# Attention units of 128 tokens: the first four computed whole, the later ones as two chunks of 64

## The chip, the cores and the metric

The kernel runs on one core of one Trainium2 chip. The core has a matrix engine (PE, with its weight loads shown apart as PEld), a vector engine (DVE), a scalar engine (ACT), a general engine (POOL) and queues that issue transfers (SP's and ACT's are used here). The metric is the device time of one execution in microseconds (us).

## The reference

Three stages follow each other. In the attention stage (4 sequences of 576 tokens, 8 heads of 64), each head's score matrix is multiplied by a fixed mask that decays with distance, and there is no softmax. The 2304 rows of its output then pass through two feed-forward layers of width 2048, one with SiLU and one with a squared ReLU.

```python
scores = scale * np.matmul(q, k.transpose(0, 1, 3, 2))
Dmat = np.where(rel >= 0, gamma[:, None, None] ** rel[None, :, :], 0.0)
x = np.matmul(scores * Dmat[None, :, :, :], v)     # then (tokens, 512)
h = x @ moe_w_in;  x = (h / (1 + np.exp(-h))) @ moe_w_out
h = np.maximum(x @ moe2_w_in, 0.0);  out = (h * h) @ moe2_w_out
```

Since the mask is a power of the distance, the attention of a chunk of tokens is a masked product inside the chunk plus the query times a state, a 64x64 matrix for each head that sums the decayed keys times values of all chunks before it in the sequence.

## The kernel before

**Feed-forward.** Weights and activations are split into a high and a low part, and each product is three matmuls (`mm3`, L74). Tokens go in five blocks of 512, 384, 384, 512 and 512. For each layer, block j and slice f of 16, `gemm1` makes `ph`, `gate` makes `gh` (ACT) and `gl` (DVE, L448), and `gemm2` of the slice two iterations earlier adds to `acc`. The work stands in the order in which the main loop (L561 to L598) writes it. Each iteration has two halves, and what is put in `later` is written at the next `flush`, one half on.

**Weights.** The first layer's 32 weight parts are converted on the chip while block 0 runs. One step of `conv_to` works on three parts: `conv_c` (ACT, L121), `conv_a` (ACT, L101 and L102), `conv_b` (DVE, L107 to L109) and `conv_d` (DVE, L125, `wl`). Five steps lie in the startup, and the main loop writes two for each iteration of block 0, ahead of that half's `flush`. The second layer's weights are converted in the same way much later.

**Attention.** The 18 units of 128 tokens (L is 64, C is 128) are all computed alike. `scores` makes `P` with 16 matmuls for the 64x64 tiles of the matrix engine, 128 columns each (L257). `mask` multiplies `P` by the table `Tm` into `rf` (DVE, L265, 1024 columns). `scale_q` (POOL, L273, two operations) multiplies the query by decay factors, and `decayed_state` multiplies the old state (POOL, L287). `values` adds into `Q` the query times the old state (8 matmuls, L306, 64x64 tiles, 128 columns), the masked scores times the values (8 matmuls, L306, all 128 rows, 128 columns), and the new part of the state (8 matmuls, L325, 64 columns). `high` copies to `xh` (ACT, L333), `new_state` adds the state (DVE, L294), and `low` makes `xl` (DVE, L333). `prep_k` multiplies the keys by a table before L325 reads them, on ACT with 8 operations (L247), in the first four units half on POOL. A matmul of 32-bit data leaves two records in the trace.

A sequence has nine chunks of 64, so a unit can span two sequences. `place` gives a chunk's place in its sequence. At place 0 there is no state yet, and at place 8 none has to be handed on. Unit 4 has places 8 and 0, unit 13 likewise; units 8 and 17 end on place 8; unit 9 begins on place 0.

Units 0 to 3 lie in the startup (`first_units`, an order written out by hand). Of the other 14, units 4 to 6 lie between the matmuls of block 0, and 7 to 17 between those of blocks 1 to 3. Each comes as two visits in the matrix engine's order, `scores_step` and, some halves later, `values_step`, which also writes `prep_k` of the next unit. `prep_k` of unit 4 alone is written by the main loop, at i equal to 2 (L573). `P` and `Q` of these units share one PSUM buffer.

Of the kernel before, what the change touches and what calls it, by code (L numbers as in the profile page):

```python
# [7 lines left out]
F32 = mybir.dt.float32  # L8
# [7 lines left out]
B, H, S, D = 4, 8, 576, 64  # L16
NT, DM, DFF = B * S, H * D, 2048
C = 128
# [20 lines left out]
def kernel(  # L39
# [118 lines left out]

    x_t = {}
    block_of = []
    for j, n in enumerate(BLOCKS):
        block_of += [(j, i * C) for i in range(n // C)]

# [1 line left out]
    raw = {}  # L168
    rf_t = {}
    S_at = {}  # L170
    FOUR = ((0, 0), (1, 1), (0, 1), (1, 0))

    cs = cp.tile([128, 1024 + 512 + 8 + 4 + 4], F32, name="cs")
    dummy = cp.tile([128, 1], F32, name="dummy")
    tabs = cs[:, 0:1024], cs[:, 1024:1536]
    Tm = tabs[0].rearrange("p (a e t) -> p e a t", a=4, e=2)
    Tq = tabs[1].rearrange("p (a t) -> p a t", a=4)
    Tkn, dec, gam = cs[:, 1536:1544], cs[:, 1544:1548], cs[:, 1548:1552]

    def load_consts(part):  # L180
        c0, n = ((12, 1024), (12 + 1024, 512))[part]
        nc.scalar.dma_start(out=tabs[part], in_=cst[:, c0 : c0 + n])

    def cut_consts(part):


        if part == 0:
            last = tabs[0].rearrange("p (h t) -> p h t", h=8)[:, :, C - 1]
            nc.scalar.activation(Tkn, last, ACTF.Copy, scale=8.0)
        else:  # L190
            nc.scalar.activation(gam, Tq[:, :, 1], ACTF.Copy, scale=8.0)
            for a in range(4):
                nc.scalar.activation(Tq[:, a], Tq[:, a], ACTF.Copy, scale=gam[:, a : a + 1])
            nc.scalar.activation(dec, Tq[:, :, C - 1], ACTF.Copy, scale=8.0)

    ap_ctx = ExitStack()
    ap = ap_ctx.enter_context(tc.tile_pool(name="ap", bufs=4))
# [3 lines left out]
    def att_psum(startup, name):  # L201
        pool, tag = ps_a, "a"
        if startup:
            pool, tag = [(ps_a, "a"), (ps_s, "s"), (ps_s, "s"), (ps_s, "s")][ps_n[0] % 4]
            ps_n[0] += 1
        return pool.tile([128, 2, 512], F32, tag=tag, name=name)
# [10 lines left out]
            for g in range(NG):  # L217
                queue.dma_start(out=raw[u][g], in_=att[NG * u + g])

    def dims(u, a, e, first, t0, t1):  # L220

        c0 = first + a % 2 * C
        return raw[u][a // 2][HALF[e], c0 + t0 : c0 + t1]

    def toks(u, a, e, first, p):

        c0 = first + (2 * a + e) % 4 * D
        return raw[u][a // 2][p, c0 : c0 + D]

    def place(u, b):  # L230

        return (2 * u + b) % PER

    def own(u):

        return slice(0, C) if place(u, 1) else HALF[1]
# [12 lines left out]
    P_of, Q_of = {}, {}  # L249

    def scores(u, startup):
        P_of[u] = P = att_psum(startup, "P")
        for a in range(4):
            for e, b in FOUR:
                o = P[HALF[b], e, a * C : a * C + C]
                k, q = dims(u, a, e, 768, b * L, b * L + L), dims(u, a, e, 0, 0, C)
                mm(o, k, q, start=True, stop=True)  # L257

    def mask(u):
        if u < n_start:  # L260
            rf = wp.tile([128, 1024], F32, tag="w", name="rf")
        else:
            rf = ap.tile([128, 1024], F32, tag="rf", name="rf", bufs=1)
        rf_t[u] = rf = rf.rearrange("p (e a t) -> p e a t", e=2, a=4)
        nc.vector.tensor_mul(rf, P_of.pop(u).rearrange("p e (a t) -> p e a t", a=4), Tm)  # L265
        if place(u, 1) == 0:
            nc.gpsimd.memset(rf[HALF[0], :, :, L:C], 0.0)

    def scale_q(u):
        if place(u, 0):  # L270
            for g in range(NG):
                q = raw[u][g][:, 0:256].rearrange("p (a t) -> p a t", a=2)
                nc.gpsimd.tensor_mul(q, q, Tq[:, 2 * g : 2 * g + 2])  # L273

    def scores_step(u):
        scores(u, False)
        mask(u)
        scale_q(u)
        decayed_state(u)

    def decayed_state(u):

        if place(u, 1) == PER - 1:
            return
        S_at[u + 1] = new = ap.tile([128, 4, D], F32, tag="S", name="S", bufs=2)
        if place(u, 0) and place(u, 1):
            nc.gpsimd.tensor_mul(new, S_at[u], dec.unsqueeze(2).to_broadcast([128, 4, D]))  # L287

    def new_state(u):
        if place(u, 1) == PER - 1:  # L290
            return
        new, add = S_at[u + 1], Q_of[u][:, 1, 0:256].rearrange("p (a d) -> p a d", a=4)
        if place(u, 0) and place(u, 1):
            nc.vector.tensor_add(new, add, new)  # L294
        else:
            nc.vector.tensor_copy(new, add)

    def values(u, startup):

        Q_of[u] = Q = att_psum(startup, "Q")  # L300
        o = Q[:, 0].rearrange("p (a t) -> p a t", a=4)
        kv = Q[:, 1, 0:256].rearrange("p (a d) -> p a d", a=4)
        started = set()

        def add(e, w, a, b, last):
            mm(w, a, b, start=e not in started, stop=last)  # L306
            started.add(e)

        parts = ((0, C),) if place(u, 1) else ((0, L), (L, C))
        if place(u, 0):  # L310
            t1 = parts[0][1]
            for a in range(4):
                for e in range(2):
                    add(e, o[HALF[e], a, 0:t1], S_at[u][HALF[e], a], dims(u, a, e, 0, 0, t1), False)
        rf = rf_t.pop(u)
        for a in range(4):
            for e in range(2):
# [3 lines left out]
        if place(u, 1) < PER - 1:  # L321
            p = own(u)
            for a in range(4):
                for e in range(2):
                    mm(kv[HALF[e], a], toks(u, a, e, 256, p), toks(u, a, e, 512, p), start=True, stop=True)  # L325
# [5 lines left out]
        xh, xl = (x[:, :, t0 : t0 + C] for x in x_t[j])  # L331
        raw.pop(u)
        return lambda: nc.scalar.copy(xh, o), lambda: nc.vector.tensor_sub(xl, o, xh)  # L333

    def values_step(u):
        high, low = values(u, False)
        later.append(lambda: (high(), new_state(u), later.append(low)))
        if u + 1 < NU:
            prep_k(u + 1)
        load(u + 2)  # L340

    def first_units():


        high, low = {}, {}

        def val(u):
            high[u], low[u] = values(u, True)

        cut_consts(0)  # L350
        cut_consts(1)
        conv_a(0)
        scores(0, True)
        mask(0)
        decayed_state(0)
        prep_k(0)
        conv_b(0)
        val(0)
        conv_c(0)
        conv_d(0)  # L360
        conv_a(1)
        new_state(0)
        high[0]()
        conv_b(1)
        low[0]()
        prep_k(1)
        scores(1, True)
        scale_q(1)
        mask(1)
        decayed_state(1)  # L370
        conv_c(1)
        conv_d(1)
        scores(2, True)
        val(1)
        scale_q(2)
        prep_k(2)
        conv_a(2)
        new_state(1)
        high[1]()
        mask(2)  # L380
        decayed_state(2)
        low[1]()
        conv_b(2)
        scores(3, True)
        val(2)
        scale_q(3)
        prep_k(3)
        new_state(2)
        high[2]()
        mask(3)  # L390
        decayed_state(3)
        conv_c(2)
        low[2]()
        conv_a(3)
        val(3)
        load(n_start, nc.scalar)
        conv_d(2)
        new_state(3)
        high[3]()
        conv_b(3)  # L400
        low[3]()
        conv_a(4)
        conv_n[0] = 5


    g_t = {}
# [105 lines left out]


    nb = len(BLOCKS)
    u_end = [sum(BLOCKS[: j + 1]) // C for j in range(nb)]
# [138 lines left out]
```

## Time and profile before

| | us |
|---|---|
| runs | 880.62, 881.86, 882.60 |
| median | 881.86 |
| profiled execution | 883.38 |
| its span, first to last instruction | 881.4 |
| PE busy in it | 867.9 (98%) |
| DVE busy | 368.8 (42%) |
| ACT busy | 351.5 (40%) |
| POOL busy | 38.5 (4%) |

The span of the profiled execution is 2.0 us shorter than its time, and its time is 1.5 us above the median. A busy PE is a mean over the whole span; the stages differ, and what an engine waited for has to be read in each of them. The startup ends at about 28.7 us, block 0 runs to 127.5, blocks 1 to 4 of the first layer follow, and attention ends at 381.5.

### The profile page before, as it was taken

Reading aid. Unit: us, or ns where it says so; the run is one execution under the profiler, and the core shown is the slowest. Engines: PE = TensorE matmul, PEld = TensorE weight load, DVE = VectorE, ACT = ScalarE, POOL = GpSimd, SP = SyncE. Lnnn points to the kernel's source line nnn. Section 1 sums busy time; section 2 is a strip of 40 time slices with the busy share of each in tenths; the row PEclk is TensorE's granted clock in tenths of the full one; section 3 lists DMA queues with packets and bytes.
Section 4 is the critical chain, followed back from the end, with each engine's and each line's share of the span. In section 5 each row is a group of like instructions: output and inputs, shape, how many; then the busy total and the mean of one; then the engine's idle time right before and its main releaser. Section 6 shows DMA issues by size and latency. Waiting matters only on the chain.

```text
span 881.4 us, 12560 instructions
## 1 busy us (share of the span) xinstructions
PE 867.9 (98%) x5186; PEld 747.7 (85%) x5186; DVE 368.8 (42%) x590; ACT 351.5 (40%) x705; POOL 38.5 (4%) x55
## 2 busy tenths in 40 slices
PE   7999999999999999999999999999999999999998
PEld 5878889999999888888888888899999888888886
DVE  4799972212222222115666777532233332323222
ACT  5687863223242222325565656322222222222221
POOL 3101100000000010000000000000000000000000
PEclk8999999999999999999999999999999999999999
DMA  9555621112112113004323432020020010001001
GB/s 349 188 181 196 223 96 48 48 49 84 49 49 94 39 49 120 1 1 147 140 97 107 175 129 80 0 84 1 1 84 1 1 67 17 1 1 48 1 1 48
DMA packets 21656, 68.17 MB, mean 77 GB/s; under 512 B 2400, under 2 KB 4192, under 8 KB 21216
## 3 DMA queue, kind: packets, MB, share of 16 engines
q1 hardware_dynamic: 16272, 54.14, 17.0%
q10 hardware_dynamic: 5328, 13.24, 4.2%
q8 instruction: 40, 0.66, 0.3%
q14 instruction: 16, 0.13, 0.0%
HBM read 57.93 MB, written 9.44 MB: 76 GB/s over the span
## 4 chain that ended last, share of the span: by engine, by line
PE 94%; DVE 0%; ACT 0%; issue 0%
PE acc L74 45%; PE ph L74 44%; PE Q L306 3%; PE P L257 2%; PE Q L325 1%; DVE gl L448 0%; DVE y L490 0%; ACT y L488 0%
## 5 line engine op out<-in xcount | busy, mean ns | idle before, releaser
L74 PE MATMUL ph<-xh,wh 128*128 128x512 f32 (+2 forms) x648 | 238.6, 368 | 0.0
L74 PE MATMUL ph<-xh,wl 128*128 128x512 f32 (+2 forms) x648 | 237.3, 366 | 0.0
L74 PE MATMUL ph<-xl,wh 128*128 128x512 f32 (+2 forms) x648 | 237.1, 366 | 0.0
L448 DVE TENSOR_TENSOR gl<-sg,gh 128x512 fp32r<-128x512 f32 (+1 forms) x160 | 104.3, 652 | 205.1 <-ACT gh L447 205.1
L74 PEld LDWEIGHTS ph<-xh,wh 128*128 128x128 f32 x648 | 121.6, 188 | 17.4 <-issue 0.7
L74 PEld LDWEIGHTS ph<-xl,wh 128*128 128x128 f32 x648 | 121.7, 188 | 15.8
L74 PEld LDWEIGHTS ph<-xh,wl 128*128 128x128 f32 x648 | 121.7, 188 | 14.8
L443 DVE SCALAR_TENSOR_TENSOR sg<-ph,sg 128x512 f32<-128x512 f32 (+1 forms) x80 | 51.0, 638 | 198.4 <-ACT sg L442 198.4
L442 ACT ACTIVATE sg<-ph 128x512 f32<-128x512 f32 (+1 forms) x80 | 44.4, 555 | 211.7 <-PE ph L74 210.0
L440 ACT ACTIVATE sg<-ph 128x512 f32<-128x512 f32 (+1 forms) x80 | 44.3, 554 | 202.2 <-PE ph L74 202.2
L74 PE MATMUL acc<-gl,wh 128*128 128x512 f32 (+1 forms) x320 | 118.5, 370 | 1.8 <-DVE gl L448 1.8
L74 PE MATMUL acc<-gh,wh 128*128 128x512 f32 (+1 forms) x320 | 119.9, 375 | 0.0
L74 PE MATMUL acc<-gh,wl 128*128 128x512 f32 (+1 forms) x320 | 118.3, 370 | 0.0
L447 ACT CAST gh<-sg 128x512 fp32r<-128x512 f32 (+1 forms) x160 | 92.4, 578 | 53.2 <-DVE sg L443 50.6
L74 PE MATMUL acc<-wh,gl 128*128 128x512 f32 x288 | 112.7, 391 | 0.0
L74 PE MATMUL acc<-wl,gh 128*128 128x512 f32 x288 | 112.6, 391 | 0.0
L74 PE MATMUL acc<-wh,gh 128*128 128x512 f32 x288 | 112.0, 389 | 0.0
L74 PEld LDWEIGHTS acc<-gh,wh 128*128 128x128 f32 x320 | 60.3, 189 | 9.8 <-issue 1.7
L74 PEld LDWEIGHTS acc<-gl,wh 128*128 128x128 f32 x320 | 60.4, 189 | 9.6 <-DVE gl L448 2.3
L74 PEld LDWEIGHTS acc<-gh,wl 128*128 128x128 f32 x320 | 60.5, 189 | 7.8
L74 PEld LDWEIGHTS acc<-wh,gl 128*128 128x128 f32 x288 | 54.0, 188 | 11.4
L74 PEld LDWEIGHTS acc<-wh,gh 128*128 128x128 f32 x288 | 54.1, 188 | 10.4
(46 smaller groups left out, 652.0 us busy)
## 6 DMA issues: line engine op xcount, KB each, us to landing
wr<-w SPq DMA_DIRECT2D x64, 512.0 KB, 3.5
raw<-att SPq DMA_DIRECT2D x32, 512.0 KB, 4.3
x<-y ACTq DMA_DIRECT2D x12, 256.0 KB, 4.4
xr<-x ACTq DMA_DIRECT2D x3, 1024.0 KB, 4.8
out<-y SPq DMA_DIRECT2D x10, 256.0 KB, 2.2
out<-y ACTq DMA_DIRECT2D x7, 256.0 KB, 2.3
x<-y ACTq DMA_DIRECT2D x8, 192.0 KB, 2.0
xr<-x ACTq DMA_DIRECT2D x2, 768.0 KB, 4.3
```

Source lines behind the costliest of these rows:

```text
L74: mm(o, a, b, start=first and i == 0, stop=last and i == n - 1)
L257: mm(o, k, q, start=True, stop=True)
L306: mm(w, a, b, start=e not in started, stop=last)
L325: mm(kv[HALF[e], a], toks(u, a, e, 256, p), toks(u, a, e, 512, p), start=True, stop=True)
L440: nc.scalar.activation(s, ph, ACTF.Silu)
L442: nc.scalar.activation(s, ph, ACTF.Relu)
L443: nc.vector.scalar_tensor_tensor(s, ph, 0.0, s, op0=ALU.max, op1=ALU.mult)
L447: nc.scalar.copy(gh, s)
L448: later.append(lambda: nc.vector.tensor_sub(gl, s, gh))
```

## The change

Units 0 to 3 keep the form they had, in functions of their own (`unit_scores`, `unit_mask`, `unit_scale_q`, `unit_decayed`, `unit_values`, `unit_state`). Units 4 to 17 are computed as two chunks of 64. All their matmuls have 64 rows, 64 columns of weights and 64 columns of data. In `scores` there are 16 for `P` and up to 16 more for the state's new parts, which stood in `values`. In `values` there are up to 16 with the two chunks' states and 16 with the masked scores. `FOUR` is the order in which the four tiles of the matrix engine are used.

`mask` has 512 columns instead of 1024. A unit has two `new_state` additions on DVE, and between them the decayed state `dS` on POOL. Half of the masked products goes to `x1`, which ACT copies out (`xs`) and DVE adds back in two operations on 64 partitions (`whole`), before `xh` is made. In units 4 to 6 `prep_k` now has its first half on POOL. The tables of 64 are cut on ACT by six operations (`cut_consts(2)`). One step of `conv_to` is written ahead of the first gates, at the end of `first_units`.

```diff
 def prep_k(u):
     for g in range(NG):
-        w = Tkn[:, 4 * g : 4 * g + 4]
-        if g == 0 and u < n_start:
+        w = (Tkn_u if u < n_start else Tkn)[:, 4 * g : 4 * g + 4]
+        if g == 0 and u < u_end[1]:
...
 def scores(u, startup):
     for a in range(4):
         for e, b in FOUR:
-            o = P[HALF[b], e, a * C : a * C + C]
-            k, q = dims(u, a, e, 768, b * L, b * L + L), dims(u, a, e, 0, 0, C)
-            mm(o, k, q, start=True, stop=True)
+            o = P[HALF[b], e, a * L : a * L + L]
+            mm(o, dims(u, a, e, b, 768), dims(u, a, e, b, 0), start=True, stop=True)
+    for a in range(4):
+        for e, b in FOUR:
+            if place(u, b) < PER - 1:
+                o = P[HALF[e], b, 256 + a * D : 256 + a * D + D]
+                mm(o, toks(u, a, e, b, 256), toks(u, a, e, b, 512), start=True, stop=True)
...
+def new_state(u, b):
+    n, i = place(u, b), 2 * u + b
+    if n == PER - 1:
+        return
+    new = ap.tile([128, 4, D], F32, tag="S", name="S", bufs=3)
+    add = P_of[u][:, b, 256:512].rearrange("p (a d) -> p a d", a=4)
+    if n == 0:
+        nc.vector.tensor_copy(new, add)
+    else:
+        nc.vector.tensor_add(new, add, dS[0])
+    S_at[i + 1] = new
+    if n + 1 < PER - 1:
+        dS[0] = ap.tile([128, 4, D], F32, tag="dS", name="dS", bufs=1)
+        nc.gpsimd.tensor_mul(dS[0], new, dec.unsqueeze(2).to_broadcast([128, 4, D]))
...
 def scores_step(u):
     scores(u, False)
     mask(u)
     scale_q(u)
-    decayed_state(u)
+    new_state(u, 0)
+    later.append(lambda: new_state(u, 1))
...
 def values(u, startup):
+    for b in range(2):
+        if place(u, b):
+            for a in range(4):
+                for e in range(2):
+                    sg = S_at[2 * u + b][HALF[e], a]
+                    add(e, o[HALF[e], a, b * L : b * L + L], sg, dims(u, a, e, b, 0), None, False)
     for a in range(4):
-        for e in range(2):
-            for t0, t1 in parts:
-                v = toks(u, a, e, 512, slice(0, C))
-                add(e, o[HALF[e], a, t0:t1], v, rf[:, e, a, t0:t1], a == 3 and t1 == C)
...
+        for e, b in FOUR:
+            v = toks(u, a, e, b, 512)
+            if e == b:
+                add(e, o[HALF[e], a, b * L : b * L + L], v, rf[HALF[b], e, a], None, a == 3)
+            else:
+                mm(x1[HALF[e], a], v, rf[HALF[b], e, a], start=True, stop=True)
+    xs = ap.tile([128, 4, L], F32, tag="xs", name="xs", bufs=1)
+    nc.scalar.copy(xs, x1)
+    def whole():
+        for e, p in enumerate(HALF):
+            b = 1 - e
+            oc = o[p, :, b * L : b * L + L]
+            if place(u, b):
+                nc.vector.tensor_add(oc, oc, xs[p])
+            else:
+                nc.vector.tensor_copy(oc, xs[p])
+        nc.scalar.copy(xh, o)
+    return whole, lambda: nc.vector.tensor_sub(xl, o, xh)
...
     conv_n[0] = 5
+    conv_to(0, 6)
+    cut_consts(2)
```

What this moves is shown at three places. PE at the first visit of unit 4, before the change (`L257` are the scores, `[waits ...]` names whose signal a row waits for):

```order
L257 MATMUL P<-raw 64x128 [waits DMAHW5_49]
L257 MATMUL P<-raw 64x128 x7
L257 MATMUL P<-raw 64x128 [waits DMAHW6_49]
L257 MATMUL P<-raw 64x128 x7
L74 MATMUL acc<-gh,wh 128x512 [waits Activation_49]
L74 MATMUL acc<-gl,wh 128x512 [waits DVE_49]
```

The first `gemm2` follows the scores at once. The same place on PE in the changed kernel (`L265` are the scores, `L270` the new parts of the state):

```order
L265 MATMUL P<-raw 64x64 [waits DMAHW5_49]
L265 MATMUL P<-raw 64x64 x7
L265 MATMUL P<-raw 64x64 [waits DMAHW6_49]
L265 MATMUL P<-raw 64x64 x7
L270 MATMUL P<-raw 64x64 [waits Pool_49]
L270 MATMUL P<-raw 64x64 x3
L270 MATMUL P<-raw 64x64 [waits Activation_49]
L270 MATMUL P<-raw 64x64
L270 MATMUL P<-raw 64x64 [waits Activation_49]
L270 MATMUL P<-raw 64x64
L74 MATMUL acc<-gh,wh 128x512
```

The new parts of the state moved into this visit, with waits for POOL and ACT, whose work is `prep_k` of unit 4.

ACT from the second of the first two gates (`L440`, `L447`) to `prep_k` of unit 4 (`L247`), before the change; `L121`, `L101` and `L102` are one step of the conversion:

```order
L440 ACTIVATE sg<-ph 128x512
L447 CAST gh<-sg 128x512
L121 CAST wh<-t 128x512
L101 ACTIVATE t<-wr 128x512
L102 ACTIVATE wr<-wr 128x512
L121 CAST wh<-t 128x512
L101 ACTIVATE t<-wr 128x512
L102 ACTIVATE wr<-wr 128x512
L121 CAST wh<-t 128x512
L101 ACTIVATE t<-wr 128x512
L102 ACTIVATE wr<-wr 128x512
L247 ACTIVATE raw<-raw,cs 128x64 x8
```

Three steps stand between the gates and `prep_k`. The same place on ACT in the changed kernel, from the last of the six cuts on (a gate is `L528` and `L535`, `prep_k` is `L255`):

```order
L206 ACTIVATE cs<-cr 128x4
L528 ACTIVATE sg<-ph 128x512
L535 CAST gh<-sg 128x512
L528 ACTIVATE sg<-ph 128x512
L535 CAST gh<-sg 128x512
L121 CAST wh<-t 128x512
L101 ACTIVATE t<-wr 128x512
L102 ACTIVATE wr<-wr 128x512
L121 CAST wh<-t 128x512
L101 ACTIVATE t<-wr 128x512
L102 ACTIVATE wr<-wr 128x512
L255 ACTIVATE raw<-raw,cs 128x64 x4
```

One step moved to a place ahead of the cuts and of both gates, two are left between the gates and `prep_k`, and `prep_k` has four operations here.

DVE at the end of block 0, where unit 6 is finished, before the change (`L294` is its state, `L333` its `xl`):

```order
L125 TENSOR_TENSOR wl<-t,wh 128x512 [waits Activation_49] x2
L448 TENSOR_TENSOR gl<-sg,gh 128x512 [waits PE_49]
L294 TENSOR_TENSOR S<-Q,S 128x256 [waits Activation_49,Pool_49]
L333 TENSOR_TENSOR xl<-Q,xh 128x4x128
L448 TENSOR_TENSOR gl<-sg,gh 128x512 [waits PE_49,Activation_49]
```

The state stands ahead of `xl`. The same place on DVE in the changed kernel (`L343` are the two additions of `whole`, `L348` is `xl`):

```order
L125 TENSOR_TENSOR wl<-t,wh 128x512 [waits Activation_49] x2
L536 TENSOR_TENSOR gl<-sg,gh 128x512 [waits PE_49]
L343 TENSOR_TENSOR Q<-Q,xs 64x4x64 [waits PE_49]
L343 TENSOR_TENSOR Q<-Q,xs 64x4x64 [waits DVE_49]
L348 TENSOR_TENSOR xl<-Q,xh 128x4x128 [waits Activation_49]
L536 TENSOR_TENSOR gl<-sg,gh 128x512 [waits PE_49,Activation_49]
```

The state left this place, two additions came, and `xl` now waits for ACT, whose `xh` itself waits for these additions.

## Rows read from the trace of the kernel before

**Rows 1.** The page, part 2: DVE's busy tenths in 40 slices of the span

```profile
DVE  4799972212222222115666777532233332323222
```

**Rows 2.** Timeline, PE, unit 10 (start, length, line, names, records)

```profile
214.35 1.10 PE L257 MATMUL P<-raw 64*64 64x128 f32 x32
215.38 0.44 PE L74 MATMUL ph<-xh,wh 128*128 128x384 f32 x1
...
223.91 1.09 PE L306 MATMUL Q<-raw,S 64*64 64x128 f32 x16
224.93 1.09 PE L306 MATMUL Q<-rf,raw 128*64 128x128 f32 x16
225.85 0.63 PE L325 MATMUL Q<-raw 128*64 128x64 f32 x16
226.42 0.45 PE L74 MATMUL ph<-xh,wh 128*128 128x384 f32 x1
```

**Rows 3.** Groups by line, PE (records, busy us, mean ns of one, idle before)

```profile
L325 PE MATMUL Q<-raw 128*64 128x64 f32 x224 | 9.3, 228 | 0.0
```

**Rows 4.** Timeline, PE, second visits of units 8 and 13

```profile
175.88 1.09 PE L306 MATMUL Q<-raw,S 64*64 64x128 f32 x16
...
177.93 0.45 PE L74 MATMUL ph<-xh,wh 128*128 128x384 f32 x1
...
279.53 0.68 PE L306 MATMUL Q<-raw,S 64*64 64x64 f32 x16
...
281.88 0.44 PE L74 MATMUL acc<-gh,wh 128*128 128x384 f32 x1
```

**Rows 5.** Timeline, PE and PEld, the first 0.1 us of a scores visit

```profile
188.54 0.34 PE L257 MATMUL P<-raw 64*64 64x128 f32 x4
...
188.53 0.21 PEld L257 LDWEIGHTS P<-raw 64*64 64x64 f32 x8 [0.25 <-issue]
```

**Rows 6.** Timeline, all engines, unit 4's first visit (brackets: idle before, what ended it)

```profile
37.61 0.69 DVE L125 TENSOR_TENSOR wl<-t,wh 128x512 fp32r<-128x512 f32 x1 [3.91 <-ACT wh L121]
...
38.50 1.10 PE L257 MATMUL P<-raw 64*64 64x128 f32 x32
...
39.42 0.42 DVE L107 TENSOR_SCALAR t<-t 128x512 int32<-128x512 int32 x1
...
41.42 0.62 ACT L121 CAST wh<-t 128x512 fp32r<-128x512 f32 x1 [1.06 <-DVE t L109]
...
43.17 1.06 ACT L247 ACTIVATE raw<-raw,cs 128x64 f32<-128x64 f32 x4
```

**Rows 7.** Timeline, PE, its one wait in block 0

```profile
52.81 0.50 PE L74 MATMUL acc<-gl,wh 128*128 128x512 f32 x1 [1.84 <-DVE gl L448]
```

**Rows 8.** Windows, after that wait (length, busy PE PEld DVE ACT POOL, PEclk, DMA, GB/s)

```profile
53.55:56.97 3.42, 3.42 (x9) 2.32 (x8) 3.23 (x6) 2.84 (x5) 0.00 (x0) 0.50 0.60 199
```

**Rows 9.** Timeline, DVE and POOL, a mask, then unit 5's POOL work

```profile
46.87 1.22 DVE L265 TENSOR_TENSOR rf<-P,cs 128x1024 f32<-128x1024 f32 x1
...
74.08 2.40 POOL L273 TENSOR_TENSOR raw<-raw,cs 128x256 f32<-128x256 f32 x2 [23.80 <-PE P L257]
74.65 1.23 DVE L125 TENSOR_TENSOR wl<-t,wh 128x512 fp32r<-128x512 f32 x1
75.81 1.22 DVE L448 TENSOR_TENSOR gl<-sg,gh 128x512 fp32r<-128x512 f32 x1
```

**Rows 10.** Timeline, POOL, unit 7, while DVE is idle

```profile
140.30 1.43 POOL L273 TENSOR_TENSOR raw<-raw,cs 128x256 f32<-128x256 f32 x2 [31.92 <-ACT sg L440]
141.68 0.62 POOL L287 TENSOR_TENSOR S<-S,cs 128x256 f32<-128x256 f32 x1
```

**Rows 11.** Timeline, DVE and PE, the end of block 0

```profile
125.49 0.42 DVE L294 TENSOR_TENSOR S<-Q,S 128x256 f32<-128x256 f32 x1
125.83 0.68 DVE L333 TENSOR_TENSOR xl<-Q,xh 128x512 fp32r<-128x512 f32 x1
...
127.70 0.34 PE L74 MATMUL ph<-xl,wh 128*128 128x384 f32 x1
```

More of the change, by code (lines that the diff above doesn't have):

```diff
@@ L163 @@
     block_of = []
+    u_end = [sum(BLOCKS[: j + 1]) // C for j in range(len(BLOCKS))]
     for j, n in enumerate(BLOCKS):
@@ L184, in cut_consts @@
     def cut_consts(part):
+        m, q = tabs
         if part == 0:
-            last = tabs[0].rearrange("p (h t) -> p h t", h=8)[:, :, C - 1]
-            nc.scalar.activation(Tkn, last, ACTF.Copy, scale=8.0)
-        else:
[L191 to L194, printed above, removed]
+            nc.scalar.activation(Tkn_u, m[:, :, C - 1], ACTF.Copy, scale=8.0)
+        elif part == 1:
+            nc.scalar.activation(gam, q[:, :, 1], ACTF.Copy, scale=8.0)
+            for a in range(4):
+                nc.scalar.activation(q[:, a], q[:, a], ACTF.Copy, scale=gam[:, a : a + 1])
+            nc.scalar.activation(dec_u, q[:, :, C - 1], ACTF.Copy, scale=8.0)
+        else:
+            for b, p in enumerate(HALF):
+                mp = m[p]
+                nc.scalar.activation(Tkn[p], mp[:, :, b * L + L - 1], ACTF.Copy, scale=8.0)
+                nc.scalar.copy(cs[p, 12:524].rearrange("p (h t) -> p h t", h=8), mp[:, :, b * L : b * L + L])
+            nc.scalar.copy(Tq, q[:, :, 0:L])
+            nc.scalar.activation(dec, q[:, :, L - 1], ACTF.Copy, scale=8.0)
@@ L218, in load, with dims, toks @@
                 queue.dma_start(out=raw[u][g], in_=att[NG * u + g])
[L220 to L225, printed above, removed]
+    def dims(u, a, e, b, first):
+        c0 = first + a % 2 * C + b * L
+        return raw[u][a // 2][HALF[e], c0 : c0 + L]
+    def toks(u, a, e, b, first):
         c0 = first + (2 * a + e) % 4 * D
-        return raw[u][a // 2][p, c0 : c0 + D]
+        return raw[u][a // 2][HALF[b], c0 : c0 + D]
     def place(u, b):
         return (2 * u + b) % PER
-    def own(u):
-        return slice(0, C) if place(u, 1) else HALF[1]
     def prep_k(u):
@@ L298, in values, with add @@
     def values(u, startup):
-        Q_of[u] = Q = att_psum(startup, "Q")
+        Q = att_psum(startup, "Q")
         o = Q[:, 0].rearrange("p (a t) -> p a t", a=4)
-        kv = Q[:, 1, 0:256].rearrange("p (a d) -> p a d", a=4)
+        x1 = Q[:, 1, 0:256].rearrange("p (a t) -> p a t", a=4)
         started = set()
-        def add(e, w, a, b, last):
+        def add(e, w, a, b, x, last):
             mm(w, a, b, start=e not in started, stop=last)
             started.add(e)
-        parts = ((0, C),) if place(u, 1) else ((0, L), (L, C))
@@ L326, in values, with values_step, unit_q, unit_kv @@
+    def values_step(u):
+        whole, low = values(u, False)
+        later.append(lambda: (whole(), later.append(low)))
+        if u + 1 < NU:
+            prep_k(u + 1)
+        load(u + 2)
+    Q_of = {}
+    def unit_q(u, a, e):
+        return raw[u][a // 2][HALF[e], a % 2 * C : a % 2 * C + C]
+    def unit_kv(u, a, e, first):
+        c0 = first + (2 * a + e) % 4 * D
+        return raw[u][a // 2][:, c0 : c0 + D]
+    def x_part(u):
         j, t0 = block_of[u]
@@ L330, in values, with unit_scores, unit_mask @@
             )
-        xh, xl = (x[:, :, t0 : t0 + C] for x in x_t[j])
+        return tuple(x[:, :, t0 : t0 + C] for x in x_t[j])
+    def unit_scores(u):
+        P_of[u] = P = att_psum(True, "P")
+        for a in range(4):
+            for e, b in FOUR:
+                o = P[HALF[b], e, a * C : a * C + C]
+                k, q = dims(u, a, e, b, 768), unit_q(u, a, e)
+                mm(o, k, q, start=True, stop=True)
+    def unit_mask(u):
+        rf = wp.tile([128, 1024], F32, tag="w", name="rf")
+        rf_t[u] = rf = rf.rearrange("p (e a t) -> p e a t", e=2, a=4)
+        nc.vector.tensor_mul(rf, P_of.pop(u).rearrange("p e (a t) -> p e a t", a=4), tabs[0].rearrange("p (a e) t -> p e a t", a=4))
@@ new lines, in unit_scale_q, with unit_decayed, unit_state @@
+    def unit_scale_q(u):
+        if u:
+            for g in range(NG):
+                q = raw[u][g][:, 0:256].rearrange("p (a t) -> p a t", a=2)
+                nc.gpsimd.tensor_mul(q, q, tabs[1][:, 2 * g : 2 * g + 2])
+    def unit_decayed(u):
+        S_at[2 * u + 2] = new = ap.tile([128, 4, D], F32, tag="S", name="S", bufs=3)
+        if u:
+            nc.gpsimd.tensor_mul(new, S_at[2 * u], dec_u.unsqueeze(2).to_broadcast([128, 4, D]))
+    def unit_state(u):
+        new, add = S_at[2 * u + 2], Q_of[u][:, 1, 0:256].rearrange("p (a d) -> p a d", a=4)
+        if u:
+            nc.vector.tensor_add(new, add, new)
+        else:
+            nc.vector.tensor_copy(new, add)
@@ new lines, in unit_values @@
+    def unit_values(u):
+        Q_of[u] = Q = att_psum(True, "Q")
+        o = Q[:, 0].rearrange("p (a t) -> p a t", a=4)
+        kv = Q[:, 1, 0:256].rearrange("p (a d) -> p a d", a=4)
+        rf = rf_t.pop(u)
+        if u:
+            for a in range(4):
+                for e in range(2):
+                    mm(o[HALF[e], a], S_at[2 * u][HALF[e], a], unit_q(u, a, e), start=a == 0, stop=False)
+        for a in range(4):
+            for e in range(2):
+                mm(o[HALF[e], a], unit_kv(u, a, e, 512), rf[:, e, a], start=u == 0 and a == 0, stop=a == 3)
+        for a in range(4):
+            for e in range(2):
+                mm(kv[HALF[e], a], unit_kv(u, a, e, 256), unit_kv(u, a, e, 512), start=True, stop=True)
+        xh, xl = x_part(u)
@@ L352, in first_units @@
         conv_a(0)
-        scores(0, True)
-        mask(0)
-        decayed_state(0)
+        unit_scores(0)
+        unit_mask(0)
+        unit_decayed(0)
         prep_k(0)
@@ L366, in first_units @@
         prep_k(1)
[L367 to L370, printed above, removed]
+        unit_scores(1)
+        unit_scale_q(1)
+        unit_mask(1)
+        unit_decayed(1)
         conv_c(1)
         conv_d(1)
-        scores(2, True)
+        unit_scores(2)
         val(1)
-        scale_q(2)
+        unit_scale_q(2)
         prep_k(2)
         conv_a(2)
-        new_state(1)
+        unit_state(1)
         high[1]()
-        mask(2)
-        decayed_state(2)
+        unit_mask(2)
+        unit_decayed(2)
         low[1]()
         conv_b(2)
-        scores(3, True)
+        unit_scores(3)
         val(2)
-        scale_q(3)
+        unit_scale_q(3)
         prep_k(3)
-        new_state(2)
+        unit_state(2)
         high[2]()
-        mask(3)
-        decayed_state(3)
+        unit_mask(3)
+        unit_decayed(3)
         conv_c(2)
```

75 lines of the change are left out of this document (24 added, 51 removed).

## The prediction

> **What bounds the kernel now.** I read the shares on the page first, then DVE by slices, then PE's timeline around the attention visits, and last the end of block 0. PE is busy 98% of the span, so after the startup time is won only where PE's own instructions get shorter, and lost only where PE comes to wait. DVE is busy 42% by the mean, but the slices say something else: three of them, from 44 to 110 us, show a 9 [rows 1]. In block 0 DVE converts the weights without a pause, and PE and DVE run at nearly the same pace there. From 150 us on DVE is nearly idle and added work on it is covered. So the change has to be priced twice, in blocks 1 to 3 on PE alone and in block 0 on PE and DVE.
>
> **The visits in blocks 1 to 3.** An ordinary unit, here unit 10, costs PE 1.03 us at its first visit, from its first matmul to the next feed-forward one (215.38 less 214.35), and 2.51 at its second [rows 2]. I count in rounds, groups of records that run side by side on different tiles. The scores are 32 records on four tiles, 8 rounds of 128 columns. L325 is 16 records on two column tiles, 8 rounds of 64 columns: it lasts 0.63, its last record 0.23 [rows 3], so seven steps take 0.40, or 0.057 each. By the same reading L306 takes (1.09 less 0.28) / 7 = 0.115 for 128 columns, of which the first step is longer. From L325's first record to the next feed-forward matmul pass 0.57.
>
> In the changed kernel the first visit has 8 rounds of scores and 8 for the state's new parts, all of 64 columns: 0.57 + 8 x 0.057 + 0.05 = 1.08. The 0.05 is for the first round of a visit, which waits for its weights, an estimate from the 0.34 of the first four records [rows 5] against some 0.28 later. The second visit has 16 rounds with the states, on two tiles as before, and 8 with the masked scores, on four: 0.57 + 16 x 0.057 + 0.05 = 1.53. The unit goes from 3.54 to 2.61, a gain of 0.93. Seven units are of this kind (7, 10, 11, 12, 14, 15, 16): 6.5 us. Units 8 and 17 have a second visit of 2.05 [rows 4], which becomes 1.53: 0.47 each with the longer first visit. Unit 9 has no state for its first chunk, 2.51 less 1.02 = 1.49 [rows 2], which becomes 1.08: 0.36. Unit 13 goes from 2.35 [rows 4] to 1.08: 1.22. Together **9.0 us** less.
>
> The trace has no round of 64 columns on four tiles. The bounds are 0.057, if four run as two do, and 0.109, the step of the scores' rounds of 128 columns ((1.10 less 0.34) / 7), if four can't go faster. I take 0.057, because at a visit's start four matmuls together last 0.34, hardly more than one, and eight weight loads lie within 0.21 [rows 5]: neither goes one after another. TensorE: Matmul & The Clock Gate of the Trainium skill (Part 1, on the measured 56 ns) states that start-to-start never drops below about 25 ns however small N is; by that four records take 0.10 us, nearly my upper bound, and it is the second rival. The x4 row speaks against it for four tiles, though not for 64 records in succession.
>
> ACT's added copy `xs` waits for PE's visit and holds up the gates behind it, and DVE's second state waits for POOL. Both are covered: ACT has about 30% work there, and the visits lie over 7 us apart. SP's transfers keep their order.
>
> **Block 0 on PE.** Unit 4 ends a sequence and begins another like unit 13: 1.2 less. Units 5 and 6 are ordinary: 1.9 less. Against that, the first visit of unit 4 now needs its keys multiplied, and `prep_k` stands on ACT behind two conversion steps. PE reaches the visit at 38.50, ACT began `prep_k` at 43.17, having waited until 41.42 for DVE's `conv_b` [rows 6]. With the step that moved ahead, this `conv_b` starts some 1.2 us earlier (below), ACT waits until 40.2, and `prep_k`, four operations of 1.06 together, ends at about 43.0. PE has its scores and half the new parts done at 39.4 and waits some 4.0 us with the whole of `gemm2` queued behind. POOL's `scale_q`, now beside this `conv_b`, can add 1.0; an earlier `conv_b` can take off 1.0.
>
> What does a wait cost besides? After its one wait in block 0, 1.84 [rows 7], the granted clock was 0.50, the 1.2 GHz level, for 3.42 us [rows 8], and PE lost half of that, 1.7. I take the same after the new wait, with 0 as the other end. The old wait and its slow stretch (1.8 + 1.7) go away, since PE comes to that place some 6 us later while DVE doesn't. PE's sum: -3.1 + 4.0 + 1.7 - 3.5 = **-0.9**.
>
> **Block 0 on DVE.** Its last duty there is `xl` of unit 6, which ends at 126.51; PE wants it at 127.70 [rows 11], so 1.19 are to spare. DVE's sum until then:
> - The step ahead: its last operation stood at 37.61 after an idle 3.91, and the next conversion began at 39.42 [rows 6]. Now it lies in the idle time, but the gates behind six cuts (some 2 us of ACT, in a gap of 3.4) come 0.5 later. Between 0 and -1.8; I take -1.2.
> - Three masks of 512 columns: from 1.22 [rows 9] to 0.68, the length of an `xl` of that width out of PSUM [rows 11]. -1.6.
> - Five state operations instead of three, 0.34 from start to start [rows 11]. +0.7.
> - Six operations of `whole`, 256 columns like a state, and each second one waits for the first, so 0.42 [rows 11]. +2.5.
> - `xl` waits for ACT's `xh`, made after `whole`: an idle 0.6 at the end.
> - POOL. While POOL did its 2.40, two DVE operations took 1.23 and 1.22 instead of 0.69, 1.07 lost, and POOL's pair took 2.40 instead of 1.43 [rows 9, 10]. DVE loses about 0.75 of POOL's undisturbed time. New on POOL are two halves of `prep_k` (0.72 each, like one `scale_q`), three decayed states (0.62 each) [rows 10], less a memset, 2.7 in all. +2.0.
>
> The sum is **+3.0**, with ends of +1 and +4.5. SBUF — State Buffer of the Trainium skill (section with the engine ports and AXI ports) calls the port pair of DVE and GpSimd an exclusive lock, where the loser fully blocks; by that the last term would be 2.7 and the sum 3.7, a longer wait by 0.7. The rows show both sides slowed, and I keep the measured share.
>
> So `xl` ends at 129.5 while PE wants it at 126.8. PE waits 2.7, in whole or in parts, and starts the last product 1.8 later than before; a slow stretch behind this wait adds 1.7. Block 0 loses **3.5**, and the wait at unit 4 is hidden in it.
>
> **Sum.** -9.0 + 3.5 = -5.5. Against the profiled execution's 883.38 (span 881.4) that is 877.9. That execution lies 1.5 over the median of the runs, 881.86, so I forecast 876.4 for the median.
>
> **The rivals.**
> - *Block 0 keeps its gain.* If DVE's sum stays under +0.3 (POOL works where DVE reads PSUM, the step ahead gives all of its 1.8), PE never waits at the end: -9.0 - 0.9, or 872.0. For it: DVE gets shorter masks. Against: every other edit adds to the engine that shows 9s [rows 1]. Chance 0.20.
> - *Four small tiles are no faster than four large ones*, and the kernel gets slower. At 0.109 a round, the rounds on four tiles (240 in blocks 1 to 3: 24 in each ordinary unit and unit 9, 16 in 8, 13 and 17) cost 0.052 more each, 12.4, so +3.4 there. Block 0 on PE becomes -3.1 + 56 x 0.052 + 4.0 + 1.7 - 3.5 = +2.0. With +5.4 the median is 887.3. It decides from 5.5 / 240 = 0.023 over 0.057, a round of 0.080. For it: 0.027 for each record is the fastest that [rows 2] show in succession. Against: [rows 5]. Chance 0.13.
> - *Block 0 loses twice what I count*: DVE's sum at +4.5, a wait at unit 6's second visit too (its `P` must be read by a state addition on DVE before `Q` can be written), and two slow stretches: +1.5 + 1.7 more, with up to 2 us for the second wait. That gives 880 to 882, no change. Chance 0.12.
>
> **How the numbers follow.** The forecast has 0.55, and its own bounds are 874 to 879. The range goes from 870 (the first rival, with the wait at unit 4 shorter) to 882 (the third), and leaves out the slower rival and a little below. What lies within 0.2%, 880.1 to 883.6, is about what a measurement of this kernel can't tell from no change. Faster has 0.55, 0.20 and a part of the third rival, 0.78; the same 0.08; slower 0.14.
>
> **What would show it.** In the changed kernel's timeline: a first visit of 1.08 and a second of 1.53 in an ordinary unit; L265 and L270 at unit 4 with an idle stretch of 4 us ended by ACT; a PE wait for `xl` at the start of block 1, and a clock of 0.50 behind each. The gain from 130 to 390 us should be 9. A first visit of 1.9 would mean the second rival; no wait at block 1 the first.

## The result and the profile after

The kernel after takes 874.67 us (median of 4, 874.15 to 875.27), the kernel before 881.99 beside it: a ratio of 0.9915, 95% interval 0.9902 to 0.9927. The forecast was 876.4, range 870 to 882. The profiled execution has 874.32 and a span of 872.5. In short, the change won 9.0 us in blocks 1 to 3, where PE is alone on the path, and gave 1.6 back in block 0, where DVE's queue sets the end.

I cut both profiles at the same three points of TensorE's work: the first feed-forward matmul, the second gemm of gate step 14 of block 0 (a little behind the start of block 1), the matmul behind the last attention visit, and the last matmul. First the kernel before by these windows (length, then busy time of PE, PEld, DVE, ACT, POOL, then PEclk, DMA share, GB/s):

```profile
28.71:129.63 100.92, 99.08 (x656) 81.85 (x653) 89.22 (x143) 77.37 (x153) 8.45 (x9) 0.98 0.50 178
129.63:381.50 251.87, 251.87 (x1953) 227.62 (x1952) 55.62 (x83) 78.17 (x190) 19.32 (x28) 1.00 0.15 55
381.50:877.15 495.65, 495.65 (x2270) 420.88 (x2268) 206.94 (x341) 179.92 (x322) 0.00 (x0) 1.00 0.15 53
```

Then the kernel after by the same points:

```profile
27.30:129.78 102.48, 96.49 (x752) 79.85 (x749) 91.75 (x151) 77.64 (x150) 13.09 (x14) 0.98 0.52 177
129.78:372.68 242.90, 242.90 (x2434) 221.79 (x2433) 60.35 (x113) 80.70 (x200) 26.61 (x38) 1.00 0.16 58
372.68:868.32 495.64, 495.64 (x2273) 421.09 (x2268) 208.30 (x343) 180.08 (x323) 0.00 (x0) 1.00 0.15 53
```

Blocks 1 to 3 are 8.97 us shorter, block 0 is 1.56 longer, the rest is the same: -7.42, against -7.3 between the medians. In block 0 PE's busy time went down by 2.59 and the block still got longer: PE now waits 5.99 us there (102.48 less 96.49), where it waited 1.84 (100.92 less 99.08). By slices DVE shows the same three 9s as in [rows 1]:

```profile
DVE  5899972222222222225666767423323332323222
```

The first feed-forward matmul comes at 27.30 instead of 28.71, and this is no effect of the change: in these two executions the kernel before had two stretches of 3.41 us at half clock in the startup and the kernel after none, and in the repeated run of the kernel after below, which had two as well, this matmul comes at 28.84. That is most of why the profiled executions differ by 9.1 us and the windows by 7.4.

The visits, for unit 10 of the kernel after, which answers to [rows 2] (timeline, PE):

```profile
212.78 0.69 PE L265 MATMUL P<-raw 64*64 64x64 f32 x32
213.29 0.65 PE L270 MATMUL P<-raw 64*64 64x64 f32 x32
213.87 0.45 PE L74 MATMUL ph<-xh,wh 128*128 128x384 f32 x1
...
222.40 1.09 PE L316 MATMUL Q<-raw,S 64*64 64x64 f32 x30
...
223.94 0.45 PE L74 MATMUL ph<-xh,wh 128*128 128x384 f32 x1
```

The first visit takes 1.09, the second 1.54. The 32 records of the scores, 8 rounds on four tiles, hold PE for 0.51 until L270 begins; less the 0.05 of a visit's first round that is 0.058 a round.

Unit 4's first visit, which answers to [rows 6] (timeline, all engines; in brackets the idle time before and what ended it):

```profile
37.09 0.69 PE L265 MATMUL P<-raw 64*64 64x64 f32 x32
...
38.32 0.62 ACT L121 CAST wh<-t 128x512 fp32r<-128x512 f32 x1 [0.85 <-DVE t L109]
...
40.57 1.05 ACT L255 ACTIVATE raw<-raw,cs 128x64 f32<-128x64 f32 x4
...
41.19 0.95 PE L270 MATMUL P<-raw 64*64 64x64 f32 x8 [3.18 <-ACT raw L255]
```

The end of block 0, which answers to [rows 11]:

```profile
124.14 0.69 DVE L125 TENSOR_TENSOR wl<-t,wh 128x512 fp32r<-128x512 f32 x1 [0.85 <-ACT wh L121]
...
125.47 0.90 DVE L343 TENSOR_TENSOR Q<-Q,xs 64x256 f32<-64x256 f32 x2
126.41 0.58 ACT L346 CAST xh<-Q 128x512 fp32r<-128x512 f32 x1 [2.29 <-DVE Q L343]
...
127.02 0.69 DVE L348 TENSOR_TENSOR xl<-Q,xh 128x512 fp32r<-128x512 f32 x1 [0.65 <-ACT xh L346]
...
127.04 0.45 PE L74 MATMUL ph<-xh,wh 128*128 128x384 f32 x1 [1.86 <-ACT xh L346]
...
127.77 0.44 PE L74 MATMUL ph<-xl,wh 128*128 128x384 f32 x1 [0.28 <-DVE xl L348]
```

PE is ready for block 1 at 125.18 and stands behind a chain of three engines' steps: `whole` on DVE, `xh` on ACT, `xl` on DVE. DVE is late there, but it also stands idle for ACT, 0.85 before `wl` and 0.65 before `xl`; so "DVE's queue" below means its instructions and these waits. The clock behind the two waits (windows; the column before the DMA share is PEclk):

```profile
41.44:44.85 3.41, 3.26 (x15) 2.48 (x12) 3.25 (x7) 3.14 (x7) 0.00 (x0) 0.50 0.40 151
...
127.74:131.15 3.41, 3.38 (x17) 3.14 (x18) 0.79 (x2) 1.41 (x3) 0.00 (x0) 1.00 0.00 0
```

It fell to 1.2 GHz behind the 3.18 at unit 4, as it had in [rows 8] behind the 1.84 of [rows 7], and not behind the 1.86 and 0.28 at block 1.

### The profile page after: what moved, and what is told of

Its sections match the earlier page's. It is cut to its first block, busy times and chain, and to the rows that moved or that the text cites. A ratio compares the mean times of both kernels' runs of the same rounds, so it can differ in the third digit from the quotient of the medians.

```text
span 872.5 us, 13730 instructions
## 1 busy us (share of the span) xinstructions
PE 856.8 (98%) x5762; PEld 740.2 (85%) x5762; DVE 377.7 (43%) x630; ACT 354.5 (41%) x713; POOL 50.9 (6%) x70
## 4 chain that ended last, share of the span: by engine, by line
PE 85%; DVE 1%; ACT 1%; issue 0%; ACTq 0%
PE acc L74 41%; PE ph L74 41%; PE Q L316 2%; PE P L265 1%; PE P L270 1%; ACT raw L255 0%; ACT wh L121 0%; PE Q L332 0%; DVE Q L343 0%; DVE t L108 0%; DVE xl L348 0%; DVE t L109 0%; DVE wl L125 0%; DVE gl L536 0%; ACT xh L346 0%
## 5 line engine op out<-in xcount | busy, mean ns | idle before, releaser
L536 DVE TENSOR_TENSOR gl<-sg,gh 128x512 fp32r<-128x512 f32 (+1 forms) x160 | 102.4, 640 | 184.7 <-ACT gh L535 184.7
L528 ACT ACTIVATE sg<-ph 128x512 f32<-128x512 f32 (+1 forms) x80 | 44.3, 553 | 176.0 <-PE ph L74 174.9
L535 ACT CAST gh<-sg 128x512 fp32r<-128x512 f32 (+1 forms) x160 | 92.4, 577 | 53.2 <-DVE sg L531 50.6
L74 PEld LDWEIGHTS acc<-wl,gh 128*128 128x128 f32 x288 | 54.1, 188 | 10.4
```

Source lines behind the costliest of these rows:

```text
L74: mm(o, a, b, start=first and i == 0, stop=last and i == n - 1)
L528: nc.scalar.activation(s, ph, ACTF.Silu)
L535: nc.scalar.copy(gh, s)
L536: later.append(lambda: nc.vector.tensor_sub(gl, s, gh))
```

## The experiments

All times in us. The windows are cut as above. Executions of one kernel differ by up to 4.7 us, and the profiled ones have different stretches at half clock, in the startup and behind waits, so I compare windows first and medians second. Beside these runs the kernel before had medians of 882.4 to 882.7.

| kernel | block 0 | blocks 1 to 3 | median |
|---|---|---|---|
| before | 100.9 | 251.9 | 882.0 |
| after | 102.5 | 242.9 | 874.7 |
| k scaling early | 103.7 | 243.0 | 878.1 |
| no step ahead | 104.0 | 242.9 | 877.2 |
| before, step ahead alone | 97.9 | 251.9 | 879.9 |
| k scaling on ACT | 102.6 | 242.9 | 874.7 |
| pairs | 102.2 | 250.8 | 882.7 |
| long pairs | 102.3 | 254.6 | 887.4 |
| attention steps early | 343.3 in all (after: 345.4) | | 873.3 |
| both early | 343.0 in all | | 873.1 |
| whole chunks in block 0 | 97.9 | 242.9 | 870.8 |
| after, repeated | 104.0 | 242.9 | 875.7 |

**What ends block 0.** My theory was that DVE's queue does. The first test takes away PE's largest wait:

```
             if i == 1:
                 load(n_start + 1)
-            if i == 2:
                 prep_k(n_start)
```

> The kernel after, with unit 4's k scaling issued one step of the main loop earlier, on ScalarE ahead of three conversion instructions instead of behind them. It asks what sets the end of block 0. Theory: VectorE's queue does, so the wait of 3.2 us at unit 4's first visit and the half-clock stretch behind it (some 1.7) go, and what TensorE gains there it loses again at the start of block 1, where its wait for unit 6's xh and xl grows from 2.2 to about 6 or 7; the time is 873.7 to 874.7 us against 874.7 of the kernel after. Rival: the wait at unit 4 stands on the path to the end, and 4.9 us go with it, to about 869.8.

The waits of PE between 28 and 140 us in this run (line waited for, total, times, longest):

```profile
PE ph L74 <- ACT sg L528: 1.9, 2, 1.0
PE ph L74 <- ACT xh L346: 1.9, 1, 1.9
PE Q L316 <- DVE S L301: 1.6, 1, 1.6
PE acc L74 <- DVE gl L536: 0.9, 1, 0.9
PE ph L74 <- DVE xl L348: 0.3, 1, 0.3
```

The wait at unit 4 is gone, and PE gives the time back all through block 0, not in one wait at its end as I wrote: 6.6 us of waits in place of 5.9. Block 0 takes 103.7, between the two profiles of the kernel after (102.5 and 104.0). DVE's `xl` of unit 6 ends 100.1 us after the first feed-forward matmul, against 100.4 in the kernel after. So the rival with 869.8 is out: the wait at unit 4 is hidden. The median is 3.4 above the top of the forecast range. The profiled execution has a half-clock stretch of 3.41 behind block 1's wait and one of 10.24 in the startup, before the first feed-forward matmul at 28.60; why the median has more of these than the kernel after isn't settled.

The second test loads DVE's queue by the step that moved, and the third gives that step to the kernel before.

```
         conv_n[0] = 5
-        conv_to(0, 6)
         cut_consts(2)
```

> The kernel after without the conversion step ahead of the first gates. Theory: the step moves VectorE's queue of block 0 forward by 1.2 to 1.6 us, and this queue ends last; without it the wait at the start of block 1 is longer by as much, and the time 875.9 to 876.3 us. Rival: the step is hidden, as the wait at unit 4 would suggest (ScalarE's k scaling is late by itself), and the time stays at 874.7.

The stretch from the first feed-forward matmul to the end of unit 6's `xl` in this run (windows):

```profile
30.27:132.18 101.91, 95.79 (x739) 78.91 (x737) 90.43 (x150) 77.18 (x150) 12.17 (x14) 0.96 0.51 174
```

Without the step `xl` of unit 6 ends 101.9 us after the first feed-forward matmul instead of 100.4 (the row for the kernel after stands below, at the fourth test), block 0 is 1.5 longer, and the median 2.5 (0.9 above the theory's range). The wait at unit 4 grew to 5.2, with 6.83 us at half clock behind it, and that at block 1 shrank to 1.0: PE loses the same time elsewhere, since DVE sets the end.

```
         conv_n[0] = 5
+        conv_to(0, 6)
```

> The kernel before with the conversion step ahead alone, whole chunks in all units. Theory: the wait of 1.84 us on gl at the beginning of block 0 goes, and with it the half-clock stretch of 3.4 us behind it (1.7 lost): 882.0 less 3.5 is 878.5 us, or up to 0.4 more if the end of VectorE's queue, which was 1.9 us ahead of TensorE at the start of block 1, now falls behind it. Rival: the wait goes but block 0 ends no earlier, since VectorE's queue sets its end in the kernel before too: 881.5 to 882.0.

```profile
27.63:125.55 97.92, 97.89 (x657) 80.72 (x653) 88.58 (x143) 77.52 (x153) 8.14 (x9) 1.00 0.54 185
```

Block 0 goes from 100.9 to 97.9, PE has no wait left in it, and no half-clock stretch: 3.0 less in the windows, 2.5 between the medians (882.4 beside it), with a ratio of 0.9973 (0.9965 to 0.9982); 3.5 had been forecast, and why a part is missing isn't settled. The rival that DVE bounds the kernel before too is out.

The fourth test asks for the price of POOL's work beside DVE.

```
-            if g == 0 and u < u_end[1]:
+            if g == 0 and u < n_start:
```

> The kernel after with the k scaling of units 4 to 6 wholly on ScalarE, as before, and nothing of it on GpSimd. It measures what GpSimd's operations cost VectorE in block 0. If they cost the 2.0 us that the prediction took (up to 1.5 of it by the two to three k scalings), VectorE's queue ends 1.0 to 1.5 us earlier and the time is 873.2 to 873.7 us. If they cost a few tenths, as the rows of the kernel after suggest, the time is 874.4 to 875.5 us: nothing won at the port, and ScalarE, with 1.05 us more for each unit, makes VectorE wait rather longer.

The time stays. From the first feed-forward matmul to the end of unit 6's `xl`, the kernel after:

```profile
27.31:127.73 100.42, 94.47 (x740) 77.83 (x737) 91.05 (x150) 77.23 (x150) 13.09 (x14) 0.98 0.53 180
```

and with the k scaling on ACT:

```profile
27.75:128.27 100.52, 96.11 (x739) 78.83 (x737) 90.20 (x150) 79.99 (x162) 9.60 (x11) 0.97 0.53 180
```

Without the three scalings POOL is busy 3.49 us less (2.96 are their own, and unit 5's `scale_q` ran shorter too), and DVE's 150 instructions take 0.85 less. On ACT the scalings cost 2.76, and DVE waits for ACT about as much longer as it won. SBUF — State Buffer of the Trainium skill (section SBUF: two separate sides) speaks of an exclusive lock in which the loser fully blocks; it names DVE operations in a two-port mode and, beside a GpSimd operation that reads SBUF, those with two SBUF inputs. If all DVE operations beside the three lost in this way, an estimate of their price is POOL's undisturbed time, 3 x 0.72 = 2.2 by [rows 10]. The rows show 0.85; which operations stood blocked, they don't show.

The run shows one thing more. Behind unit 4's wait, 3.4 here, PE runs at half clock for 6.83 us instead of 3.41, and block 0 takes 102.6 all the same: this stretch is hidden like the wait.

```profile
41.24:48.07 6.83, 6.42 (x27) 4.78 (x28) 6.48 (x12) 6.44 (x17) 0.00 (x0) 0.50 0.52 181
```

The fifth writes block 0's attention steps earlier, the last ones by four halves, so that unit 6's last operations stand ahead of conversions that PE needs later. Unit 7's first visit comes into block 0 by this as well, so the two windows are compared as a sum:

```
-                run_att(a0 + (a1 - a0) * (2 * f + half + 1) // (2 * KF - 3))
+                run_att(a0 + (a1 - a0) * (2 * f + half + 1) // (2 * KF - (3 if j else 7)))
```

> The kernel after with the attention steps of block 0 up to four half steps of the main loop earlier, so that unit 6's last result stands ahead of the last conversions (n = 30 and 31) in VectorE's queue, which TensorE needs only two gate steps later. Theory: unit 6's xl is what block 0 waits for at its end, because it stands last in VectorE's queue; it comes some 5 us earlier, the waits of 1.9 and 0.3 at the start of block 1 go, and the time is 872.0 to 872.7 us. Rival: the queue as a whole is late, and a gl or a wl of gate steps 13 to 15 is waited for instead: 874.2 to 875.

Timeline, DVE and PE, the end of block 0 in this run:

```profile
120.72 0.69 DVE L348 TENSOR_TENSOR xl<-Q,xh 128x512 fp32r<-128x512 f32 x1
...
128.21 0.33 PE L74 MATMUL ph<-xh,wh 128*128 128x384 f32 x1
```

`xl` now ends 6.8 us before PE comes, the wait at block 1 is gone, and the windows are 2.1 shorter, as the theory had it (the median 0.6 above its range). This shows the cause of that wait: the place of unit 6's last operation in DVE's queue.

> The edit of the run with unit 4's k scaling one step earlier and the earlier attention steps together. Theory: with the end of VectorE's queue relieved by some 5 us, the 4.9 us at unit 4's first visit (wait and half-clock stretch) are no longer given back in full; TensorE follows VectorE's queue through block 0 (waits of about 1 us each on ScalarE's s, whose instructions stand behind the conversions), and block 0 takes 97.5 to 99.5 us instead of 102.5: 870 to 872 us. Rival: TensorE's waits inside block 0 grow by what the end gains: 874 to 875.

With both edits only 0.3 more is won, and the expected 870 to 872 is missed. A new wait stands inside block 0 (timeline, all engines):

```profile
65.19 0.69 DVE L348 TENSOR_TENSOR xl<-Q,xh 128x512 fp32r<-128x512 f32 x1
65.34 0.62 ACT L535 CAST gh<-sg 128x512 fp32r<-128x512 f32 x1
...
65.98 0.69 PE L265 MATMUL P<-raw 64*64 64x64 f32 x32 [3.40 <-ACT gh L535]
```

PE, at unit 5's first visit, waits 3.4 and has a half-clock stretch behind it. `P` and `Q` share one buffer in PSUM, whose last reader before is unit 4's `xl`, done at 65.88; the profile names `gh`, done at 65.96. Which of them PE waited for I can't tell apart. Either way it is the backlog of DVE or ACT, met earlier.

**What block 0 loses by the chunks of 64.** Units 4 to 6 got the functions of the kernel before, with the tables of 128 tokens kept for them (their buffers are taken in an order that frees them in time):

```
-        for step in (scores_step, values_step)
+        for step in ((w_step, w_values) if u < u_end[1] else (scores_step, values_step))
```

> Units 4 to 6 as whole chunks, as before, units 7 to 17 as two chunks of 64, with the conversion step ahead; the two tables of 128 tokens are kept until unit 6. It asks what the chunks of 64 cost in block 0, where TensorE is not alone on the path. Theory: block 0 takes what it took in the kernel before with the step ahead alone (97.9 us from the first gemm to the second gemm of gate step 14, against 102.5), blocks 1 to 3 what they take in the kernel after (242.9): 874.7 less 4.6 is 870.1 us. Rival: block 0's loss has another cause than the chunks of 64 (the tables' six instructions on ScalarE, the order at the beginning), and the time stays within 1 of 874.7.

```profile
27.27:125.19 97.92, 97.79 (x655) 80.78 (x653) 88.68 (x143) 79.04 (x159) 8.69 (x10) 1.00 0.55 185
125.19:368.08 242.89, 242.89 (x2433) 221.80 (x2432) 60.35 (x113) 80.70 (x200) 26.44 (x38) 1.00 0.17 58
```

Both windows came as forecast, and the median is 870.8, a ratio to before of 0.9878 (0.9859 to 0.9897). This version beats both kernels. DVE has 3.07 less to do in block 0 than in the kernel after, its `xl` ends at the moment at which PE asks for it, and PE waits nowhere.

**What blocks 1 to 3 win.** The matmuls of scores, new states and masked scores in another order, first the two diagonal tiles, then the others:

```
+    PAIRS = [(a, e, b) for p in (FOUR[:2], FOUR[2:]) for a in range(4) for e, b in p]
...
-        for a in range(4):
-            for e, b in FOUR:
+        for a, e, b in PAIRS:
```

> The kernel after with the same matmuls of units 4 to 17 in another order: in the scores, the state updates and the products of masked scores and values, the two tiles on the diagonal run through all heads first and then the two others, so that only two tiles take turns where four did. It asks where the 9.0 us of blocks 1 to 3 come from. Theory: a round over the tiles takes about 0.06 us with two tiles as with four, so each of some 320 rounds of four (252 of them in blocks 1 to 3) becomes two: 14 to 16 us more there and up to 4 more in block 0, 889 to 895 us. Rival: the records of 64 columns are cheap by themselves, in whatever order (0.016 us each): no change, 874.7.

The same matmuls in this order give back 7.9 of the 9.0 us. So records of 64 columns are not cheap by themselves, and the rival is out. But I had forecast 14 to 16 more in blocks 1 to 3 and at least 889 for the time, which is 882.7. Unit 7's first visit in this run (timeline, PE):

```profile
139.19 0.80 PE L265 MATMUL P<-raw 64*64 64x64 f32 x26
...
139.95 0.80 PE L269 MATMUL P<-raw 64*64 64x64 f32 x27
140.69 0.44 PE L74 MATMUL acc<-gh,wh 128*128 128x384 f32 x1
```

It takes 1.50 where four tiles take 1.09, and 32 rounds one after another would take 1.9: L269's first records start while L265's last still run. Hence a run in which the pairs stay apart for longer, scores and state updates of one pair, then both of the other:

```
+        for pair in (FOUR[:2], FOUR[2:]):
             for a in range(4):
-                for e, b in FOUR:
+                for e, b in pair:
```

> The kernel after with the pairs of tiles kept apart for longer than in the first run on pairs: scores and state updates of the two diagonal tiles first, then scores and state updates of the two others. The records of the first run showed a tile taking its next record 0.058 us after its last, and the second pair beginning while the first has two to three rounds left. Theory: each tile keeps its own rhythm of 0.058 us, tiles run beside each other, and only the pair's end overlaps; an ordinary unit's first visit then takes some 0.35 us more than in the first run on pairs (2.1 against 1.76; 1.36 in the kernel after), blocks 1 to 3 about 3 to 4 us more (253.5 to 254.5 against 250.75), and the time is 885.5 to 887 us. Rival: the pairs cost what they cost by switching between them, and fewer switches make it faster than the first run on pairs: below 882.7.

```profile
140.76 0.68 PE L267 MATMUL P<-raw 64*64 64x64 f32 x16
141.28 0.46 PE L272 MATMUL P<-raw 64*64 64x64 f32 x10
...
142.04 0.63 PE L272 MATMUL P<-raw 64*64 64x64 f32 x16
142.60 0.44 PE L74 MATMUL acc<-gh,wh 128*128 128x384 f32 x1
```

The visit takes 1.84 with one change between pairs instead of three, 0.34 more than in the first run on pairs (the expectation counts both from the matmul before, some 0.27 earlier), and blocks 1 to 3 take 254.6, 0.1 above the theory's range (the median 0.4 above): the theory holds, and the rival is out. L267's 16 records, 8 rounds on two tiles, hold the first pair for 0.52 until L272, as 32 records on four tiles do for 0.51 in the kernel after. A tile takes a record each 0.058 us, whether two tiles are at work or four, and only the end of one pair overlaps with the start of the next.

**The clock behind block 1's wait.** The kernel after, once more.

> The kernel after once more, for the clock behind its waits. In the first profile the half-clock stretch followed the wait of 3.2 us at unit 4's first visit, and none followed the waits of 1.9 and 0.3 at the start of block 1, where 1.7 had been forecast. Theory: the wait at block 1 is near the edge of what brings the clock down, so another execution can show it there or not; the first gemm to the last matmul then takes 841.4 without, or some 843 with it. Rival: a wait of this length never does it here, and 841.4 comes again within 0.3. In both the median stays at 874.2 to 876.5.

PE's waits in this execution (between 28 and 140 us):

```profile
PE P L270 <- ACT raw L255: 3.2, 1, 3.2
PE ph L74 <- ACT xh L346: 1.9, 1, 1.9
PE Q L316 <- DVE S L301: 0.4, 1, 0.4
PE ph L74 <- DVE xl L348: 0.3, 1, 0.3
```

and the window behind the last of them:

```profile
129.30:132.71 3.41, 3.36 (x11) 3.36 (x12) 0.69 (x1) 0.43 (x1) 0.00 (x0) 0.51 0.00 0
```

The same waits, to a tenth, and this time PE runs at half clock behind the second too: block 0 takes 104.0 instead of 102.5, and the first feed-forward to the last matmul 842.5 instead of 841.0, as the theory had it. The six times are 874.1 to 874.4 three times and 877.0 to 877.8 three times. The profiled one, 877.41, is 3.1 above the first profile of this kernel: 1.54 are in the startup, 1.56 behind this wait. Whether the same two places separate the others isn't shown. The ratio is 0.9925 (0.9908 to 0.9942).

## Why the prediction was right, step by step

- **Blocks 1 to 3, -9.0:** -8.97. The visits of 1.08 and 1.53 came as 1.09 and 1.54, and a round on four tiles takes 0.058, the lower bound that I took. The runs on pairs show that this rests on four tiles at work together. The second rival fell with it. Start to start of the records on four tiles is 0.016 us on average. TensorE: Matmul & The Clock Gate of the Trainium skill (Part 1, on the measured 56 ns) has about 25 ns as the least; that holds here on one tile, with 58, and not across four, where the four records of a round start within 0.02 us.
- **Unit 4's wait, 4.0:** 3.2 (the prediction's own times, 43.0 less 39.4, give 3.6), with the half-clock stretch behind it as forecast, and both are hidden, as the runs with the k scaling early and on ACT show. The old wait of [rows 7] is gone.
- **DVE's sum, +3.0:** `xl` of unit 6 ends 100.4 after the first feed-forward matmul, before 97.8: +2.6. The step ahead gave 1.5 (forecast 1.2), masks, states and `whole` came within 0.3 of their terms (`whole` 0.90 a pair, 2.7 in all). Two terms were mis-sized, one each way. ACT: DVE waits 1.5 for `wh` in three places and 0.65 for `xh`, where the kernel before waited 0.6 for `wh`; that is 1.5 more, and I had 0.6. POOL: by difference some 0.8 is left for it, and I had 2.0. I took the 1.07 of [rows 9], lost by two DVE operations beside one pair of 2.40, for the price of all; a k scaling had 0.54 in that sum (0.75 x 0.72) and costs 0.28 with all that it shifts (0.85 / 3). That the sum came within 0.4 is thus in part luck: one miss made up for the other.
- **The wait at block 1, 2.7:** 1.86 and 0.28, less by 0.6, of which DVE's smaller sum is 0.4. Moving `xl` forward in DVE's queue takes it away.
- **The slow stretch behind it, 1.7:** this is the step that failed in the profiled execution: nothing was lost. In the repeated execution 1.56 was. It should have been a chance, not a term of the sum: without it block 0's loss is forecast at 1.8 (measured 1.56), with it at 3.5 (measured 3.1 in the repeat).
- **The sum, -5.5:** -7.4 in the windows. Of the 1.9 between them 1.7 are that stretch, and in the repeat, which has it, the windows give -5.9.
- **The rivals:** block 0 did not keep its gain. Of the third rival the wait at unit 6's second visit did come, with 0.54, too little to matter, and the second half-clock stretch comes and goes.

## What to carry to other kernels

When one engine is busy from end to end of a stretch, price an edit there on that engine's queue, up to its last duty, and expect waits of the others to move but not to go; an edit that pays where TensorE is alone on the path can be left out of such a stretch (870.8 instead of 874.7). Where matmuls have few columns, issue them in turn over all tiles: the same ones, two tiles at a time, took away 7.9 of 9.0 us. Put a possible half-clock stretch behind a wait into the range and not, as a certainty, into the sum.

## What the runs showed of the hardware

A tile of 64x64 takes its next fp32 record of 64 columns 0.058 us after the last, and four tiles do so side by side, so 32 records take 0.51 us; records of another tile pair start while the earlier pair's last rounds run (a visit of 32 rounds in pairs took 1.50 us and not 1.9). The same waits of TensorE, 1.9 and 0.3 us, were followed by 3.41 us at half clock in one execution of a kernel and by none in another. Three scalings on POOL, 2.96 us in all, cost DVE 0.85 with what they shift.
